# Moving two GpSimd memsets of a fused attention and MLP kernel to the wait for x, and fixing the order of its first layer-norm operations

## Chip, cores and metric

One NeuronCore of a Trainium2 chip. The metric is the device time of one execution in microseconds (us), lower is better. "Span" is the part of an execution that the profile covers; in every profiled run here it is 1.7 to 1.8 us shorter than the time. A run is called slow when it lies over 1.5% above the fastest of the same kernel; ratios use the fast runs alone.

## The reference, cut to what matters

```python
x = A_x                                   # 1 x 2048 x 448, bf16
xn = layernorm(x)
s = linear_attention(xn, wqkv, wo)        # 16 heads of 28
g = silu((relu(xn @ w1 + b1) ** 2) @ w2 + b2)
return x + s * g
```

## The kernel before

The kernel builds a list of operations with their dependencies and estimated durations. A list scheduler then chooses the order on VectorE (DVE), ScalarE (ACT) and GpSimd (POOL); the order on TensorE (PE) and on the DMA-issuing queue of SyncE (SP) is that of the program. Every engine's program then holds its list in that order, with semaphores to wait on.

To start PE before the layer norm is known, the first eight tiles of `x @ w1` use raw x. The norm is applied afterwards, by adding a small matmul (the "augmenting" matmuls, L901) to their accumulators. Its operands are statistics rows, made on VectorE:

```python
        pr.hot = -100.0                  # rising priorities for this group
        for si in range(4):
            ln_stats(si)                 # L511 bn_stats, L513 bn_aggr
        stat_rows()                      # L844, L851, L864, L868: the rows; ACT: rstd, sdev
        ln(0, 4, stats=False, rstd=False)  # L537 normalise, L546 copy, DMA transposes of xn
        pr.hot = None
# ... (cut)
        rt = row_transpose()             # PE transposes rows, L892 copies them to SBUF
# ... (cut)
        aug([H0[i] for i in range(4)], range(4), True)      # L901
# ... (cut)
        load_k("sp", w_qkv, A_wqkv, "wq", 0, D)   # SP queue, behind the first transposes
        load_w1(3, "sp", "sp")
        load_x(8, 12)                    # x for tiles 8 to 11: VectorE waits for it later
        ln(4, 8, lead=3, hold=[rt])
```

GpSimd meanwhile writes constants. `hmask` and `kvm` are needed only in the last third of the kernel, `ehd` too:

```python
        def late_constants():
            hv = hmask[:, :].rearrange("p (b j) -> p b j", b=HC)
            pool(lambda e, _: e.memset(hv, 1.0), ["hmask"])
            # ... two affine_selects on hmask; zmask: one memset, eight affine_selects (cut)
            pool(lambda e, _: e.memset(kvm[:, :, :], 0.0), ["kvm"], dur=1.0)   # 128 x 1792 bf16
            pool(lambda e, _: e.memset(ehd[:, :], 0.0), ["ehd"], dur=0.5)
            # ... four affine_selects on ehd, 128 x 448 bf16 each (cut)
```

Of the kernel before, what the change touches and what calls it, by code (L numbers as in the profile page):

```python
# [28 lines left out]
class Op:  # L29
    def __init__(self, eng, emit, reads, writes, dur, alts, nbytes):  # L30
        self.eng, self.emit, self.dur, self.alts, self.nbytes = eng, emit, dur, alts, nbytes
        self.reads, self.writes = list(reads), list(writes)
        self.raw, self.deps, self.succ = set(), set(), []
        self.start = self.end = None
        self.seq = None
        self.late = 1e9
        self.prio = None
        self.sync = None
        self.fence = False
        self.fixed = 0.0  # L40
        self.hold = ()


class Program:
# [14 lines left out]
    def add(self, eng, emit, reads=(), writes=(), dur=0.2, alts=(), nbytes=0):  # L59
        reads = [p for r in reads for p in self.aliases.get(r, (r,))]  # L60
        op = Op(eng, emit, reads, writes, dur, alts, nbytes)
        op.lead = self.lead
        if self.hot is not None:
            self.hot += 0.01
            op.prio = self.hot
        for t in op.reads:
            w = self.writer.get(t)
            if w is not None:
                op.raw.add(w)
            self.readers.setdefault(t, []).append(op)  # L70
        for t in op.writes:
            w = self.writer.get(t)
            if w is not None and w is not op:
                op.deps.add(w)
            for r in self.readers.get(t, ()):
                if r is not op:
                    op.deps.add(r)
            self.writer[t] = op
            self.readers[t] = [r for r in self.readers.get(t, ()) if r is op]
        op.raw.discard(op)  # L80
        op.deps |= op.raw
        for d in op.deps:
            d.succ.append(op)
        self.ops.append(op)
        return op

    def schedule(self):
# [29 lines left out]
        pend = {e: [] for e in self.ENGINES}  # L117
# [4 lines left out]
        def ready(op):  # L122
            r = 0.0
            for d in op.deps:
                if d.end is None:
                    return None
                r = max(r, d.end + LAT)
            for d in op.hold:
                if d.end is None:
                    return None  # L130
                r = max(r, d.start)
            return r
# [14 lines left out]
        while n:  # L147
            best = None
            for e in self.ENGINES:
                if e in fixed:  # L150
                    if not pend[e]:
                        continue
                    op = pend[e][0]
                    r = ready(op)
                    if r is None:
                        continue
                    new = [b for b in op.writes if isinstance(b, Buf) and b.bank is None]
                    banks = []
                    if new:
                        times = sorted(  # L160
                            (bank_time(b), b) for b in range(PSUM_BANKS) if bank_time(b) is not None
                        )
                        if len(times) < len(new):
                            continue
                        banks = [b for _, b in times[: len(new)]]
                        r = max(r, times[len(new) - 1][0])
                    st = max(r, free[e])
                    cand = (st, 0, op, e, banks, op.dur)
                else:
                    cands = []  # L170
                    for op in pend[e]:
                        r = ready(op)
                        if r is not None:
                            cands.append((max(r, free[e]), op))
                    for o in ops:
                        if o.end is None and o.alts:
                            for ae, ad in o.alts:
                                if ae == e:
                                    r = ready(o)
                                    if r is not None:  # L180
                                        cands.append((max(r, free[e]), o))
                    keep = []
                    for st, op in cands:
                        if op.alts:
                            mine = op.dur if op.eng == e else dict(op.alts)[e]
                            others = [(op.eng, op.dur)] + list(op.alts)
                            r = ready(op)
                            if any(
                                max(r, free[x]) + dx < st + mine - 1e-9 for x, dx in others if x != e
                            ):  # L190
                                continue
                            keep.append((st, op, mine))
                        else:
                            keep.append((st, op, op.dur))
                    if not keep:
                        continue
                    m = min(keep, key=lambda k: k[0])
                    st, op, du = min(
                        (k for k in keep if k[0] <= m[0] + min(0.6 * m[2], 0.02 + max(0.0, 0.3 * (m[1].late - k[1].late)))),
                        key=lambda k: k[1].late,  # L200
                    )
                    cand = (st, 1, op, e, [], du)
                if best is None or cand[0] < best[0] - 1e-12:
                    best = cand
            st, _, op, e, banks, du = best
            if op.eng != e:
                pend[op.eng].remove(op)
                op.eng = e
            else:
                pend[e].remove(op)  # L210
            for b, k in zip([b for b in op.writes if isinstance(b, Buf) and b.bank is None], banks):
                b.bank = k
                if bank_last[k] is not None:
                    self.bankdeps.setdefault(op, []).extend(users[bank_last[k]])
                bank_last[k] = b
            op.start = st
            if op.fixed:
                free[e] = st + op.dur
                op.end = st + op.dur + op.fixed
            elif op.nbytes:  # L220
                free[e] = st + op.dur
                s2 = max(dma_free, st + 1.9)
                dma_free = s2 + op.nbytes / 330e3
                op.end = dma_free + 0.7
            else:
                op.end = st + du
                free[e] = op.end
            order[e].append(op)
            n -= 1
# [63 lines left out]
def bass_recurrent_scan__linear_attn_block__dense_activation_squared_relu__prompt_kernel(  # L293
    nc, A_x, A_wqkv, A_wo, B_x, B_w1, B_b1, B_w2, B_b2, out
):
    with ExitStack() as es:
# [3 lines left out]
        add = pr.add  # L300
# [4 lines left out]
        hmask = sb("hmask", [P, PD], f32)  # L305
# [51 lines left out]
        def pool(fn, writes, reads=(), dur=0.3):  # L357
            add("pool", fn, reads, writes, dur)
# [45 lines left out]

        def late_constants():
            hv = hmask[:, :].rearrange("p (b j) -> p b j", b=HC)
            pool(lambda e, _: e.memset(hv, 1.0), ["hmask"])
            select(hv, "hmask", [[-DH, HC], [0, DH]], 0, 1, 0.0)
            select(hv, "hmask", [[DH, HC], [0, DH]], DH - 1, -1, 0.0)
            pool(lambda e, _: e.memset(zmask[:, :, :], 1.0), ["zmask"])  # L410
            for view, pat, base in (
                (zmask[:, 0:3, :], [[P, 3], [-DH, 32]], 0),
                (zmask[:, 3, :], [[-DH, 32]], 384),
                (zmask[:, 4, :], [[-DH, 32]], 320),
            ):
                select(view, "zmask", pat, base, 1, 0.0)
                select(view, "zmask", [[-a, n] for a, n in pat], DH - 1 - base, -1, 0.0)
            select(zmask[:, 3, :], "zmask", [[0, 32]], 63, -1, 0.0)
            select(zmask[:, 4, :], "zmask", [[0, 32]], -64, 1, 0.0)
            pool(lambda e, _: e.memset(ones[:, :], 1.0), ["ones"], dur=0.1)  # L420
            pool(lambda e, _: e.memset(kvm[:, :, :], 0.0), ["kvm"], dur=1.0)
            pool(lambda e, _: e.memset(ehd[:, :], 0.0), ["ehd"], dur=0.5)
            ev = ehd[:, :].rearrange("p (h j) -> p h j", h=NH)
            for g in range(NG):
                select(ev, "ehd", [[-1, NH], [0, DH]], -32 * g, 1, 1.0, ALU.not_equal, dur=0.6)
# [958 lines left out]
```

## Time and profile before

| | before |
|---|---|
| time, median | 150.86 us of 3 runs (150.5 to 150.94); with one more run 150.71 |
| span of the profile | 149.6 us (that execution took 151.34 us) |
| PE busy | 96% of the span |
| first operation on the statistics rows, L844 | 1.72 us for 128x32 elements |
| augmenting matmuls, L901 | start at 12.43 us |
| first transposes of xn on the SP queue | issued at 11.37 us |
| first matmuls of the second weight, L1106 | start at 38.62 us |

The profiled execution was slower than the median of the kernel's other executions.

The page of the profile of before: the span, the busy times, and PE and VectorE in 40 slices of 3.7 us, in tenths.

```profile
span 149.6 us, 2937 instructions
PE 143.4 (96%) x1164; PEld 71.4 (48%) x1165; DVE 99.7 (67%) x232; ACT 79.2 (53%) x149; POOL 37.2 (25%) x56
...
PE   7998998999899999999999999999999999999990
...
DVE  3799749999988899647999701059693616226353
```

PE, busy for 96% of the span, is the bound, so only its gaps can be won. The view of who waited for whom, for PE (time in total, times, longest):

```profile
PE pb L1223 <- DVE bsel L380: 1.1, 1, 1.1
PE pb L901 <- DVE scr L892: 0.7, 1, 0.7
PE pb L665 <- ACT pqT L643: 0.6, 1, 0.6
PE pb L1106 <- DVE r L722: 0.5, 1, 0.5
```

The timeline of VectorE (start, duration, engine, line, operation, out<-in):

```profile
8.13 1.72 DVE L844 TENSOR_SCALAR rows<-mv 128x32 bf16<-128x32 f32 x1
9.88 0.23 DVE L851 SCALAR_TENSOR_TENSOR rows<-mv,rows 128x16 bf16<-128x16 f32 x1
9.98 0.19 DVE L864 CAST rows<-sdev 128x16 bf16<-128x16 f32 x1
10.06 0.48 DVE L537 TENSOR_SCALAR xn<-x_tok,mv,rstd 128x448 bf16<-128x448 bf16 x1
10.46 0.21 DVE L868 TENSOR_TENSOR rows<-sdev,rows 128x16 bf16<-128x16 f32 x1
...
22.47 0.63 DVE L511 BATCH_NORM_STATS2 st<-x_tok 128x6 f32<-128x448 bf16 x1 [2.02 <-DMA x_tok<-in_A_x_dram]
...
36.81 1.75 DVE L722 TENSOR_TENSOR r<-r 128x512 bf16<-128x512 bf16 x5
```

and of GpSimd:

```profile
8.20 1.59 POOL L421 MEMSET kvm<- 128x1792 bf16 x1
```

L844 runs from 8.13 to 9.85, the memset from 8.20 to 9.79. That an operation of only 32 elements takes 1.72 us and ends 0.06 us after a memset on another engine suggests that it was waiting for it. At 22.47 VectorE had waited 2.02 us for the load of x's tiles 8 to 11. The SP queue shows why that load comes late; it is the fourth group behind the first transposes, and the queue has hardly a gap:

```profile
11.37 2.72 SPq L551 DMA_TRANSPOSE xT<-xn  x2
14.13 1.79 SPq L430 DMA_DIRECT2D w_qkv<-in_A_wqkv_dram  x3
15.96 0.59 SPq L430 DMA_DIRECT2D w<-in_B_w_dram  x1
16.60 1.76 SPq L430 DMA_DIRECT2D w_1r<-in_B_w_dram  x2
18.40 0.58 SPq L430 DMA_DIRECT2D x_tok<-in_A_x_dram  x1
```

### The profile page before, as it was taken

The page shows a single profiled execution, that of the slowest core. Times are in us where ns is not written, and L with a number is a line of the kernel's source. Part 1 is how long each engine was busy: PE and PEld are TensorE (multiplying, and loading weights), DVE is VectorE, ACT ScalarE, POOL GpSimd, SP SyncE. Part 2 cuts the span into 40 slices and gives each one's busy share as a digit, 9 for nine tenths or more (in the row PEclk, how much of TensorE's full clock was granted, in tenths as well). Part 3 has the DMA queues.
Part 4 walks back from the last instruction along what each step waited for, and adds up shares of the span by engine and source line. Part 5 has one row for each costly group of instructions (what it writes and reads, how often), then busy time and mean ns, then how long its engine had stood idle before and what let it go on. Part 6 is the DMA issues. An engine that isn't in the chain of part 4 may idle for free.

```text
span 149.6 us, 2937 instructions
## 1 busy us (share of the span) xinstructions
PE 143.4 (96%) x1164; PEld 71.4 (48%) x1165; DVE 99.7 (67%) x232; ACT 79.2 (53%) x149; POOL 37.2 (25%) x56
## 2 busy tenths in 40 slices
PE   7998998999899999999999999999999999999990
PEld 7962443554344445444444454454444544545450
DVE  3799749999988899647999701059693616226353
ACT  1525889679876796078969822897511020310200
POOL 7870023255000155000550000000000917208100
PEclk9999999999999999999999999999999999999999
DMA  4996889991330650000000000000000110201112
GB/s 119 330 288 127 197 183 216 334 326 36 67 73 0 40 105 0 0 0 4 0 2 4 2 0 0 4 0 0 0 0 4 61 61 32 91 4 61 61 61 61
DMA packets 17995, 11.06 MB, mean 74 GB/s; under 512 B 9469, under 2 KB 17597, under 8 KB 17982
## 3 DMA queue, kind: packets, MB, share of 16 engines
q1 hardware_dynamic: 17420, 10.42, 28.5%
q10 hardware_dynamic: 562, 0.46, 0.9%
q8 instruction: 9, 0.15, 0.4%
q14 instruction: 4, 0.03, 0.1%
HBM read 6.95 MB, written 1.84 MB: 59 GB/s over the span
## 4 chain that ended last, share of the span: by engine, by line
PE 84%; DVE 12%; ACT 2%; issue 0%; DVEq 0%
PE pb L1106 29%; PE pb L746 19%; PE pb L665 6%; PE pb L920 6%; PE pb L687 6%; PE pb L1173 6%; PE pb L1223 3%; DVE xn L537 3%; DVE r L722 2%; PE pb L745 2%; DVE pk L655 2%; PE pb L1209 1%; DVE rows L844 1%; PE pb L926 1%; PE pb L1006 1%; DVE pk L648 1%
## 5 line engine op out<-in xcount | busy, mean ns | idle before, releaser
L1106 PE MATMUL pb<-w,r 128*128 128x448 bf16 x224 | 44.3, 353 | 0.5 <-DVE r L722 0.5
L746 PE MATMUL pb<-xT,w 64*128 64x512 bf16 x288 | 37.8, 376 | 0.0
L717 ACT ACTIVATE r<-pb,b1f 128x512 bf16<-128x512 f32 x48 | 30.1, 691 | 6.5 <-PE pb L746 6.4
L1106 PEld LDWEIGHTS pb<-w,r 128*128 128x128 bf16 x224 | 21.1, 98 | 21.7 <-issue 2.2
L675 POOL TENSOR_TENSOR zacc<-zacc,pk 128x448 f32<-128x448 f32 x13 | 14.4, 1105 | 41.4 <-DVE pk L655 38.1
L1146 ACT ACTIVATE gbuf<-gbuf 128x448 bf16<-128x448 bf16 x15 | 8.5, 581 | 29.7 <-DVE gbuf L1136 29.7
L1162 POOL TENSOR_TENSOR obuf<-obuf,x_tok 128x448 bf16<-128x448 bf16 x12 | 12.0, 1035 | 48.6 <-DVE obuf L1156 48.6
L746 PEld LDWEIGHTS pb<-xT,w 64*128 64x128 bf16 x288 | 14.3, 94 | 16.1 <-issue 0.4
L722 DVE TENSOR_TENSOR r<-r 128x512 bf16<-128x512 bf16 x35 | 17.4, 532 | 2.3 <-ACT r L717 2.2
L1136 DVE TENSOR_TENSOR gbuf<-pb,b2b 128x448 bf16<-128x448 f32 x11 | 6.9, 625 | 13.7 <-PE pb L1106 13.6
L1156 DVE TENSOR_TENSOR obuf<-pb,gbuf 128x448 bf16<-128x448 f32 (+2 forms) x17 | 9.4, 592 | 7.3 <-PE pb L1173 4.7
L665 PE MATMUL pb<-w_qkv,xT 64*128 64x448 bf16 x112 | 13.3, 349 | 0.6 <-ACT pqT L643 0.6
L1089 DVE TENSOR_TENSOR pqT<-pqT,pb 128x512 bf16<-128x512 bf16 x12 | 7.4, 680 | 8.6 <-PE pb L1066 8.6
L723 ACT ACTIVATE r<-r 128x512 bf16<-128x512 bf16 x21 | 12.6, 637 | 0.0
L511 DVE BATCH_NORM_STATS2 st<-x_tok 128x6 f32<-128x448 bf16 x16 | 9.1, 611 | 3.2 <-DMA x_tok<-in_A_x_dram 3.2
L687 PE MATMUL pb<-xT,w_qkv 64*128 64x512 bf16 x84 | 11.0, 376 | 0.0
L655 DVE SCALAR_TENSOR_TENSOR pk<-pb,pk 128x448 bf16<-128x448 f32 x16 | 9.8, 622 | 0.4
L643 ACT ACTIVATE pk<-pb 128x448 bf16<-128x448 f32 x16 | 7.8, 541 | 4.0 <-PE pb L665 4.0
L920 PE MATMUL pb<-pk,xn 128*128 128x448 bf16 x48 | 9.4, 353 | 0.0
L746 PE MATMUL pb<-xT,w_1r 64*128 64x512 bf16 x48 | 9.2, 376 | 0.0
L665 PEld LDWEIGHTS pb<-w_qkv,xT 64*128 64x128 bf16 x112 | 5.5, 94 | 6.6 <-ACT pqT L643 1.0
L655 DVE SCALAR_TENSOR_TENSOR pqT<-pb,pqT 128x512 bf16<-128x512 f32 x12 | 8.2, 689 | 0.3
(122 smaller groups left out, 143.7 us busy)
## 6 DMA issues: line engine op xcount, KB each, us to landing
out_dram<-obuf SPq DMA_DIRECT2D x15, 112.0 KB, 1.7
w<-in_B_w_dram SPq DMA_DIRECT2D x1, 1568.0 KB, 8.7
x_tok<-in_A_x_dram SPq DMA_DIRECT2D x3, 448.0 KB, 4.6
w_qkv<-in_A_wqkv_dram SPq DMA_DIRECT2D x3, 336.0 KB, 6.4
w<-in_B_w_dram SPq DMA_DIRECT2D x2, 384.0 KB, 5.7
x_tok<-in_A_x_dram SPq DMA_DIRECT2D x2, 224.0 KB, 3.1
w_o<-in_A_wo_dram SPq DMA_DIRECT2D x1, 392.0 KB, 8.0
w<-in_B_w_dram ACTq DMA_DIRECT2D x1, 384.0 KB, 4.5
```

The lines of the kernel that those rows point to most:

```text
L655: lambda e, _: e.scalar_tensor_tensor(out=slot, in0=ps(buf)[:, 0:n], scalar=1.0 + 1e-6, in1=slot, op0=ALU.add, op1=ALU.max),
L665: return e.matmul(ps(b)[:, 0:D], xT[rw, si, c, :], w_qkv[rw, c, D : 2 * D], start=start, stop=stop)
L675: lambda e, _: e.tensor_tensor(out=o[:, :], in0=pk[:, 0, :] if i == 1 else zacc[:, :], in1=pk[:, i, :], op=ALU.add),
L687: return e.matmul(ps(b)[:, 0:512], w_qkv[rw, c, m * P : (m + 1) * P], xT[rw, 4 * g : 4 * g + 4, c, :], start=start, stop=stop,)
L717: rl = lambda e, _: e.activation(out=slot, in_=ps(b)[:, 0:512], func=AF.Relu, bias=b1f[:, fi : fi + 1])
L722: return e.tensor_tensor(out=slot, in0=slot, in1=slot, op=ALU.mult)
L723: return e.activation(out=slot, in_=slot, func=AF.Square)
L746: return e.matmul(ps(b)[:, 0:512], lhs, xT[rw, 4 * g : 4 * g + 4, c, :], start=start, stop=stop)
L920: last = e.matmul(ps(b)[:, 0:D], xn[:, si, c * P : (c + 1) * P], pk[:, si, :], start=(si == 0), stop=(si == NT - 1),)
L1106: last = e.matmul(ps(bb[fi >= 8])[:, 0:D], r2[:, fi, si * P : (si + 1) * P], w_2[:, fi, :], start=(fi == 0 and part is None) or (g == 0 an ...
L1156: "dve", lambda e, _: e.tensor_tensor(out=ob, in0=ps(b)[:, 0:w], in1=gs, op=ALU.mult),
L1162: lambda e, _: e.tensor_tensor(out=ob, in0=ob, in1=x_tok[:, si, lo:hi], op=ALU.add),
```

## The change

The intent: the kvm memset (1.59 us) and hmask's memset should run while VectorE still waits for x. A second part, the "rank" rule, makes VectorE and ScalarE take the operations of the first group in program order. Before, the scheduler could pass one by another.

```diff
+        self.rank = None
...
         if self.hot is not None:
             self.hot += 0.01
-            op.prio = self.hot
+            op.prio = op.rank = self.hot
...
+                    first = min((o.rank for o in pend[e] if o.rank is not None), default=None)
                     for op in pend[e]:
-                        r = ready(op)
+                        r = ready(op) if op.rank is None or op.rank == first else None
...
-            pool(lambda e, _: e.memset(hv, 1.0), ["hmask"])
+            add("pool", lambda e, _: e.memset(hv, 1.0), [], ["hmask"], 0.2).prio = -40.0
...
-            pool(lambda e, _: e.memset(kvm[:, :, :], 0.0), ["kvm"], dur=1.0)
+            add("pool", lambda e, _: e.memset(kvm[:, :, :], 0.0), [], ["kvm"], 1.0).prio = -50.0
```

The change adds two lines, so L844 of before is L846 of after, L901 is L903, L1106 is L1108, and so on. The text keeps the numbers of before.

## The prediction

> **What bounds the kernel now.** The page gives PE 96% busy of a 149.6 us span, and its slices show PE at 8 to 9 tenths from the first slice to the last but one. So the time changes only by PE's idle gaps. The view of PE's waits lists four: 1.1 us at the start (warm-up matmuls wait for a VectorE memset), 0.7 us at 12.43 (the augmenting matmuls, L901, wait for the VectorE copy of the transposed statistics rows, L892), 0.6 us at 25.10 (a bank that ScalarE has to empty), 0.5 us at 38.62 (L1106 waits for VectorE's squares, L722). The chain of waits in order of time runs on VectorE without a break from 6.39 to 12.38 and hands to L901 at 12.43: only here can the change act directly.
>
> **The suspect.** In that chain the first row operation (L844, 128x32 elements) takes 1.72 us, 8.13 to 9.85. Its neighbours of 128x16 take 0.19 to 0.23. GpSimd's memset of kvm (128x1792 bf16) runs 8.20 to 9.79, 1.59 us: the row operation ends 0.06 us after it. [...] about 1.5 us of the row operation is waiting. Likewise L537 (normally 0.39 us) has one of 1.19 us at 34 to 36.9, beside GpSimd adds of 1.1 us.
>
> **What the change moves.** The kvm memset, and hmask's (0.19 us), go to about 1.8 us, behind ident, rows and eps5, which the priorities still put first. They end at about 3.6, about when the first x tile's statistics begin (3.49). The tiny L393 (0.24 us at 1.83) will probably be held by the memset until about 3.4, and the statistics start 0.1 to 0.2 later: free, as VectorE then idles 1.1 us before 5.97. The zmask and ehd selects slide by about 1.8 us and now lie beside the row operations, until about 10.4. I think they hold VectorE little: L537 at 10.06 took 0.48 beside a hmask select, 0.09 over its usual time.
> The rank rule puts each aggregation behind its statistics and the last row operation before the first normalisation. I estimate 0.1 us lost for each of two dependent pairs.
>
> **On the critical path.** The first row operation falls to about 0.25 us. VectorE's rows and normalisations come about 1.3 us earlier. But PE is busy until 11.77 with work that doesn't need them (col sums, tails, row transposes at 10.73, L745), and csl waits for a ScalarE copy that ends at 10.64. L901 then starts at about 11.8 instead of 12.43: of 1.5 us saved on VectorE, 0.65 us reaches PE. The first transposes of xn are issued at about 10.1 instead of 11.37, so the SP queue, back to back from there to past 25 us, and the x loads behind it come about 1 us earlier (VectorE waits 2.0 us for one at 22.47). That may take some tenths off the gap at 38.62. Everything else shifts along.
>
> **Prediction.** 150.86 - 0.65 - 0.15 = 150.05 us; 8 in 10: 149.3 to 150.8. Faster by over 2%: 0.03; within 2%: 0.96; slower: 0.01.
>
> **Signs.** L844 at 0.2 to 0.4 us; kvm's memset over before 3.7; L393 over 1 us; PE's 0.7 us wait for L892 gone or under 0.1; L901 near 11.8; SP's first transposes near 10.1; the gap at 38.62 not over 0.5.
>
> **What would make it wrong.** The ehd selects (0.67 us each) holding L844, L851 and the normalisations as the memset did, which gives the gain back; the altered VectorE order moving a later square or bank release; the gap at 38.62 growing by what was won, because VectorE's load from 28 to 38 us sets it.

The sum is 150.86 less 0.65 for L901 and 0.15 for the earlier load of x, 150.05. The "about 1.5 us" of waiting is the estimate, the 1.72 us of L844 less the 0.19 to 0.23 us of its neighbours.

## The result, and the profile after

| | before | after |
|---|---|---|
| time, median | 150.71 us of 4 runs (150.5 to 150.94) | 150.12 us of 4 runs (149.97 to 150.45) |
| ratio after / before | | 0.9964, 95% interval 0.994 to 0.9988 |
| the same ratio (e6 below, chip 9) | | 0.997, interval 0.9947 to 0.9993 |
| span of the profile | 149.6 | 148.4 |
| L844, L864 | 1.72, 0.19 us | 0.72, 0.67 us |
| L901 starts | 12.43 | 11.98 |
| first transposes issued | 11.37 | 10.91 |
| L1106 starts | 38.62 | 37.42 |

A ratio is the mean time of one kernel's fast runs over that of the other's of the same rounds, so it isn't quite the ratio of the medians that are quoted.

The page of after:

```profile
span 148.4 us, 2936 instructions
PE 143.2 (97%) x1164; PEld 71.6 (48%) x1165; DVE 100.8 (68%) x231; ACT 79.5 (54%) x150; POOL 37.2 (25%) x56
...
PE   7999999999999999999999999999999999999990
...
DVE  6899859899988899458999510069683617226343
```

What PE waited for:

```profile
PE pb L1225 <- DVE bsel L382: 1.1, 1, 1.1
PE pb L903 <- DVE scr L894: 0.3, 1, 0.3
PE pb L1108 <- issue: 0.2, 1, 0.2
```

VectorE:

```profile
1.83 1.91 DVE L395 TENSOR_SCALAR rm<-ident 128x4 f32<-128x4 bf16 x1 [0.25 <-POOL eps L378]
...
8.29 0.72 DVE L846 TENSOR_SCALAR rows<-mv 128x32 bf16<-128x32 f32 x1
9.05 0.23 DVE L853 SCALAR_TENSOR_TENSOR rows<-mv,rows 128x16 bf16<-128x16 f32 x1
9.15 0.67 DVE L866 CAST rows<-sdev 128x16 bf16<-128x16 f32 x1
9.86 0.23 DVE L870 TENSOR_TENSOR rows<-sdev,rows 128x16 bf16<-128x16 f32 x1
...
21.44 0.63 DVE L513 BATCH_NORM_STATS2 st<-x_tok 128x6 f32<-128x448 bf16 x1 [1.47 <-DMA x_tok<-in_A_x_dram]
...
35.91 1.42 DVE L724 TENSOR_TENSOR r<-r 128x512 bf16<-128x512 bf16 x4
```

GpSimd:

```profile
1.78 1.59 POOL L423 MEMSET kvm<- 128x1792 bf16 x1
...
6.67 3.10 POOL L370 TENSOR_SCALAR_AFFINE_SELECT ehd<-ehd 128x448 bf16<-128x448 bf16 x4
```

The SP queue:

```profile
10.91 2.80 SPq L553 DMA_TRANSPOSE xT<-xn  x2
...
17.39 0.59 SPq L432 DMA_DIRECT2D x_tok<-in_A_x_dram  x1
```

The hold of the memset is gone from the rows. But the affine selects of ehd, which slid from 5.0 to 8.1 us into 6.7 to 9.8 us, now lie beside them: L844 takes 0.72 us and L864 0.67 us, about 0.5 us each over their free times (0.20 us each, e11 below). The third select ends at 8.96 and L844 at 9.01, the fourth at 9.77 and L864 at 9.82: the same sign as with the memset. The memset now holds the tiny L393 instead, for 1.91 us, which costs nothing here. Two gaps of PE beyond those of the rows closed too: the 0.6 us at 25.10, and most of the 0.5 us at 38.62.

### The profile page after: what moved, and what is told of

Its sections match the earlier page's. It is cut to its first block, busy times and chain, and to the rows that moved or that the text cites. A ratio compares the mean times of both kernels' runs of the same rounds, so it can differ in the third digit from the quotient of the medians.

```text
span 148.4 us, 2936 instructions
## 1 busy us (share of the span) xinstructions
PE 143.2 (97%) x1164; PEld 71.6 (48%) x1165; DVE 100.8 (68%) x231; ACT 79.5 (54%) x150; POOL 37.2 (25%) x56
## 4 chain that ended last, share of the span: by engine, by line
PE 84%; DVE 8%; DMA 3%; SPq 2%; issue 1%; ACT 0%; DVEq 0%
PE pb L1108 29%; PE pb L748 22%; PE pb L922 6%; PE pb L1175 6%; PE pb L689 5%; PE pb L667 5%; PE pb L1225 3%; DMA x_tok<-in_A_x_dram 3%; DVE st L513 3%; SPq L432 2%; PE pb L704 1%; PE pb L1211 1%; PE pb L928 1%; PE pb L1008 1%; DVE xn L539 1%; DVE pk L657 1%
## 5 line engine op out<-in xcount | busy, mean ns | idle before, releaser
L1108 PE MATMUL pb<-w,r 128*128 128x448 bf16 x224 | 44.3, 353 | 0.2 <-issue 0.2
L1108 PEld LDWEIGHTS pb<-w,r 128*128 128x128 bf16 x224 | 21.1, 98 | 21.4 <-issue 2.6
L725 ACT ACTIVATE r<-r 128x512 bf16<-128x512 bf16 x22 | 13.3, 636 | 0.0
```

What stands on the lines that cost most here:

```text
L725: return e.activation(out=slot, in_=slot, func=AF.Square)
L1108: last = e.matmul(ps(bb[fi >= 8])[:, 0:D], r2[:, fi, si * P : (si + 1) * P], w_2[:, fi, :], start=(fi == 0 and part is None) or (g == 0 an ...
```

## The experiments

Three theories. T: a GpSimd instruction holds VectorE's row operations, and moving the memset is the gain. R: the rank rule's new order is the gain. N: the waits were a chance of one profile. Kernels of one call ran on one chip: e1 to e4, e5 to e8, e9 to e12. All results were correct to the reference.

For reading all of them together, this table gives the milestones of the thirteen profiles that are of use (us from the span's start, read from the timelines): the first copy of transposed x by VectorE (L770), which marks how soon PE got going; L901; the issue of the first transposes; the end of VectorE's wait for x's tiles 8 to 11; L1106; and the span.

| profile | L770 | L901 | transposes | x there | L1106 | span |
|---|---|---|---|---|---|---|
| before | 5.97 | 12.43 | 11.37 | 22.47 | 38.62 | 149.6 |
| before, e5 | 5.65 | 12.40 | 11.35 | 22.33 | 38.53 | 149.5 |
| memsets only, e1 | 5.96 | 11.86 | 10.80 | 21.66 | 37.87 | 148.9 |
| memsets only, e9 | 5.12 | 11.22 | 10.18 | 21.32 | 37.56 | 148.5 |
| rank only, e2 | 5.20 | 12.04 | 10.99 | 21.46 | 37.40 | 148.4 |
| rank only, e10 | 5.42 | 12.02 | 10.96 | 21.87 | 37.78 | 148.8 |
| after | 5.96 | 11.98 | 10.91 | 21.44 | 37.42 | 148.4 |
| after, e6 | 5.77 | 11.56 | 10.52 | 21.42 | 37.33 | 148.3 |
| kvm split, e3 | 5.18 | 11.25 | 10.39 | 21.34 | 37.42 | 148.4 |
| kvm double, e4 | 5.02 | 13.08 | 12.03 | no wait | 40.15 | 151.1 |
| deferred, e11 | 5.96 | 11.79 | 10.16 | 21.14 | 37.34 | 148.3 |
| deferred and rank, e12 | 5.93 | 11.53 | 10.07 | 20.96 | 36.88 | 147.8 |
| deferred, x early, e8 | 5.88 | 11.48 | 9.85 | 14.48 | 37.62 | 148.6 |

Three things stand in it. The rest of the span after L1106 is 110.9 to 111.0 us in every row: all that the variants do is decided by then. L1106 comes 16.1 to 16.2 us after x is there with the old order, and 15.9 to 16.0 us with the rank rule, in all rows but e4 and e8. And L770 itself varies from 5.02 to 5.97 us between executions.

The last comes from PE's rate. PE's first matmuls (the warm-up, L1223, and the transposes of x, L763) start 107 ns apart, and from some moment on 56 ns apart. That moment lay at 6.0 us in before and after, and near 3.8 us in e4 and e9 (an estimate from the starts of the groups: 38 warm-up matmuls from 1.05 us, and the first transpose at 4.49 and 4.46 us). In e11 it had not come when the last transpose of x started near 6.25 (an estimate: the twelfth start from 5.08 us on, at 107 ns). So the 12 transposes took 1.27 us in before and 0.83 us in e4, and the moment varies by over 2.4 us between executions. What sets it isn't shown. The granted clock doesn't show it: it is recorded as 1.00 from the first matmuls on, also where these start 107 ns apart (windows view of before, after and e1 to e4; the mean of the profiled executions of e9 and e11 is 1.0).

### e1 and e9: only the memsets

```diff
 # the kernel before, with
-            pool(lambda e, _: e.memset(hv, 1.0), ["hmask"])
+            add("pool", lambda e, _: e.memset(hv, 1.0), [], ["hmask"], 0.2).prio = -40.0
-            pool(lambda e, _: e.memset(kvm[:, :, :], 0.0), ["kvm"], dur=1.0)
+            add("pool", lambda e, _: e.memset(kvm[:, :, :], 0.0), [], ["kvm"], 1.0).prio = -50.0
```

> The kernel before with the two memsets moved and without the rank rule: only GpSimd's order changes, every other engine's order is that of before. Theory T (the memset holds the first row operation until it ends): L844 falls from 1.72 us to 0.2 to 0.8 us (it may still meet an ehd select of 0.67 us), L901 starts 0.3 to 0.7 us earlier than 12.43, the time is 0.3 to 0.8 us under the kernel before, which is all or nearly all of the gain of the change. Rival R (the gain comes from the rank rule's new order on VectorE): L844 is as short, but L901 stays within 0.2 us of 12.43 and the time within 0.2 us of before.

Measured: 150.59 us median (150.03 to 151.21), ratio to before 0.9991, interval 0.9961 to 1.0021. PE's wait before L901 is gone, as T expected:

```profile
8.23 0.20 DVE L844 TENSOR_SCALAR rows<-mv 128x32 bf16<-128x32 f32 x1
8.46 0.60 DVE L851 SCALAR_TENSOR_TENSOR rows<-mv,rows 128x16 bf16<-128x16 f32 x1
...
9.33 0.67 DVE L868 TENSOR_TENSOR rows<-sdev,rows 128x16 bf16<-128x16 f32 x1
```

Here the selects hit two other operations, each with two inputs: L851 took 0.60 us and L868 0.67, against 0.23 and 0.22 in e11. The time is not lower beyond its noise.

> e1 again, on the same chip as e10 to e12, since e1's interval (0.9961 to 1.0021) told nothing. Theory T: no operation of VectorE over 0.8 us before 12 us except L393; PE's wait before L901 under 0.2 us; ratio to before 0.994 to 0.998. Rival R (the rank rule is the cause): ratio 0.999 to 1.002.

Measured: 150.65 us median (150.17 to 151.11), ratio 1.000, interval 0.9977 to 1.0024. No row operation was over 0.7 us and PE's wait was 0.17 us, as T expected; but the ratio isn't what T expected. On the time, T's claim that the memsets alone bring the gain has failed twice. In profiles with the same start (L770 at 5.96 or 5.97) e1 still has a span 0.7 us shorter than before (148.9 against 149.6).

### e2 and e10: only the rank rule

```diff
 # the kernel after, with the two memset lines of before
-            add("pool", lambda e, _: e.memset(kvm[:, :, :], 0.0), [], ["kvm"], 1.0).prio = -50.0
+            pool(lambda e, _: e.memset(kvm[:, :, :], 0.0), ["kvm"], dur=1.0)
 # (hmask likewise)
```

> The kernel after with the two memsets put back where they were: VectorE, ScalarE, PE and SP have the order of after, GpSimd that of before. Theory T: L844 is 1.4 to 1.7 us again, ending about 0.06 us after the kvm memset; L901 at 12.2 to 12.6; the time within 0.2 us of the kernel before. Rival R: L844 as long, but L901 near 12.0 and the time 0.4 to 0.8 us under before.

Measured: 150.53 us median (150.03 to 151.02), ratio 0.9987, interval 0.9958 to 1.0015. The start was an early one, so the memset (8.25 to 9.84 us) met a later operation than L844. L844 took 0.72 us, and:

```profile
8.32 1.58 DVE L866 CAST rows<-sdev 128x16 bf16<-128x16 f32 x1
```

It ends at 9.90, 0.06 us after the memset. L901 came at 12.04, the figure of R, but PE had been ready 0.72 us earlier, as T says.

> e2 again, for the same reason. Theory T: one operation of VectorE ends within 0.1 us of the kvm memset's end (9.8 to 9.9) and takes over 1.5 us; PE's wait before L901 0.6 to 1.2 us; ratio to before 0.999 to 1.002. Rival R: ratio 0.994 to 0.998.

Measured: 150.63 us median (150.37 to 151.37), ratio 1.001, interval 0.9984 to 1.0037. Again the cast took 1.58 us, and PE waited 0.78 us for L901. R fails too: the rank rule alone brings no gain in time that is clear of its noise.

### e3: the memset in four pieces

```diff
-            pool(lambda e, _: e.memset(kvm[:, :, :], 0.0), ["kvm"], dur=1.0)
+            pool(lambda e, _: [e.memset(kvm[:, c, :], 0.0) for c in range(4)][-1], ["kvm"], dur=1.0)
```

> The kernel before, with the kvm memset issued as four instructions of 448 elements at the same place, about 0.45 us each, so GpSimd writes the same bytes at the same time. [...] L844 ends within 0.1 us of the end of the first or second piece, so it takes 0.4 to 1.0 us, and L901 comes 0.3 to 0.6 us earlier than before. If VectorE is only slowed for as long as GpSimd writes[...]: L844 stays at 1.5 us or over and L901 at about 12.4.

The first outcome there is that of T: L844 is held to the end of one piece. The other is that it is slowed or held through all four. The 0.45 us for a piece is an estimate; in before the memset of ehd, as long as a piece (448 elements), took 0.47 us.

Measured: 150.32 us median (149.88 to 150.97), ratio 0.9975, interval 0.9948 to 1.0002. In this early start L844 came before the memsets and took 0.20 us. So the forecast for L844 could not be tested. The first operations that met the four pieces took 0.66 us (L864) and 0.68 us (L537), the normalisations and the copy after them 0.50 to 0.62 us, each ending within 0.17 us of the end of a piece, if the four, from 8.20 to 10.31, are taken as equally long (an estimate; they were read as one group); nothing in the group was over 0.70 us, and L901 started at 11.25. GpSimd wrote the same bytes in 2.11 us instead of 1.59. So here no operation was held through the 2.11 us of all four; VectorE got its turns in between. The time is not clear of that of before.

### e4: a memset twice as long

```diff
-        kvm = sb("kvm", [P, 4, D], bf)
+        kvm = sb("kvm", [P, 8, D], bf)      # the memset covers all of it; only half is used
```

> The kernel before with a kvm tile twice as large, so its memset is one instruction of 3584 elements, about 3.15 us; all orders as before. T: L844 takes 3.2 to 3.4 us and ends 0.06 us after the memset; VectorE has no slack after it, so L901 comes about 1.5 us later, near 13.95, and the time rises by 1.2 to 1.7 us. If the row operation is not on the path of PE, L844 grows alike but L901 and the time move by under 0.5 us.

Measured: 152.65 us median (152.23 to 152.91), ratio 1.0124, interval 1.0099 to 1.0149: 1.9 us more. The start was early, so the memset (8.26 to 11.47) met not L844 but the second normalisation:

```profile
8.46 3.14 DVE L537 TENSOR_SCALAR xn<-x_tok,mv,rstd 128x448 bf16<-128x448 bf16 x1
```

usually 0.39 us. That is T, at twice the dose. L901 came at 13.08, only 0.65 us later than in before, but e4's start was early: in e9, with as early a start and no memset in the way, L901 came at 11.22, and in e2, with the memset of 1.59 us, at 12.04. Part of the time lost in the profiled execution is of another kind, which the windows view shows (stretch, PE busy, weight loads, VectorE, ScalarE, GpSimd, then the granted PE clock, DMA share, GB/s):

```profile
12.00:14.00 2.00, 0.92 (x7) 0.41 (x8) 2.00 (x6) 0.47 (x1) 0.16 (x1) 1.00 0.37 70
14.00:16.00 2.00, 2.00 (x7) 0.73 (x5) 2.00 (x9) 1.97 (x6) 0.00 (x0) 0.51 1.03 190
16.00:18.00 2.00, 2.00 (x13) 0.28 (x13) 1.67 (x7) 0.09 (x1) 0.00 (x0) 0.63 0.82 210
```

In this execution PE waited 2.13 us for L901; after that its granted clock was 0.51 from 14 to 16 us and 0.63 from 16 to 18 us, and the nine matmuls behind L901 took 3.42 us instead of 2.12 (e1). Not every execution had this: the mean granted clock was 0.987 and 0.986 in the two that took 152.9 us, but 1.000 in the two of 152.23 and 152.30 us. The latter are still about 1.6 us above the mean of before in the same call (150.71 us), within the 1.2 to 1.7 us that T expected; about 0.6 us of the slowest two goes with the clock.

### e5 and e6: before and after again

> The kernel before, unchanged: a placebo, and a second profile of it. The profiles so far show two starts: PE's matmuls reach full rate before 5 us (e2, e3, e4) or only near 6 us (before, after, e1). Time ratio to before 0.998 to 1.002. Theory T: [...] PE's wait before L901 is 0.6 to 0.8 us in a late start, 0.8 to 1.4 us in an early one. Rival N (the wait of 0.7 us was a chance of the one profile of before): it is under 0.3 us here.

What was to be measured: an operation of VectorE that is up when the memset starts at 8.20 ends with it at 9.8 to 9.9. "Full rate" is the 56 ns from start to start of above.

Measured: ratio of before to itself 1.0005, interval 0.9977 to 1.0032. N fails: the hold is there again, and PE waited 0.66 us for L901 and 0.33 us for the transposes of the rows before it.

```profile
7.72 2.10 DVE L844 TENSOR_SCALAR rows<-mv 128x32 bf16<-128x32 f32 x1
```

L844 came up 0.4 us earlier than in the first profile, while a select was running, and still ended at 9.82, 0.06 us after the kvm memset. It was held through three GpSimd instructions in a row: the select (to 8.11), the hmask memset (8.05 to 8.24) and the kvm memset (8.17 to 9.76).

> The kernel after, unchanged, for more times of it on the same chip as the others, and a second profile. Ratio to before 0.993 to 0.999, as in the first measurement (0.9964). Theory T: no VectorE operation longer than 0.75 us before 12 us except L393 near 2 us; PE's wait before L901 is 0.2 to 0.5 us in a late start and up to 0.8 us in an early one, at least 0.3 us less than before has in the same kind of start.

Measured: 150.36 us median (150.04 to 150.63), ratio 0.997, interval 0.9947 to 0.9993. No row operation is longer than 0.45 us, and PE doesn't wait for L901 at all.

### e7 and e11: all late constants out of the start

```diff
         def late_constants():
-            # hmask, kvm and ehd: memsets and affine_selects
             # zmask and ones stay
+        def deferred_constants():
+            after = [("pk", 11)]
+            pool(lambda e, _: e.memset(kvm[:, :, :], 0.0), ["kvm"], after, dur=1.6)
+            # hmask and ehd likewise, then their affine_selects
...
         for i in range(8, 12):
             zsum(i)
+        deferred_constants()
```

> The kernel before with the kvm memset and all work on hmask and ehd moved to GpSimd's idle time near 58 us, so after about 4.5 us GpSimd does nothing until its first add near 20 us. The order of every other engine is that of before, without the rank rule. Theory T [...]: L844, L851, L864, L868 take 0.19 to 0.25 us each, L537 0.38 to 0.40; PE's wait before L901 is under 0.1 us in either start; the time is 0.3 to 0.9 us under before. If the affine selects do no harm, the result is that of e1 (time within 0.2 us of e1's).

Measured: five runs of 149.19 to 150.64 us; ratio 0.9942, interval 0.991 to 0.9974. A sixth execution, the profiled one, took 833 us. In it the matmuls of L746 took 1697 ns instead of 377, and the 38 warm-up matmuls already 12.50 us instead of 4.23 (e11), with a granted clock of 1.00 in the records. It counts as slow and is left out; its cause is open.

> e7 again, as its profile fell on an execution of 833 us. No hold left: L844, L851, L864, L868 0.19 to 0.25 us each; PE's wait before L901 under 0.1 us; the first transposes issued 0.4 to 1.0 us earlier than in after; ratio to before 0.991 to 0.997, at or under after's 0.997. A second execution far over 160 us would mean that the kernel itself, and not that execution, is at fault.

Measured: 149.93 us median (149.06 to 150.34), ratio 0.9947, interval 0.9916 to 0.9977; no slow execution among the six. VectorE in the profile (this kernel's lines are 3 higher than those of before):

```profile
8.26 0.20 DVE L847 TENSOR_SCALAR rows<-mv 128x32 bf16<-128x32 f32 x1
8.50 0.23 DVE L854 SCALAR_TENSOR_TENSOR rows<-mv,rows 128x16 bf16<-128x16 f32 x1
8.83 0.20 DVE L867 CAST rows<-sdev 128x16 bf16<-128x16 f32 x1
8.93 0.40 DVE L540 TENSOR_SCALAR xn<-x_tok,mv,rstd 128x448 bf16<-128x448 bf16 x1
9.24 0.22 DVE L871 TENSOR_TENSOR rows<-sdev,rows 128x16 bf16<-128x16 f32 x1
```

These are the free times. The start was as late as that of before (L770 at 5.96), and all orders but GpSimd's are those of before; the first transposes go out 1.2 us earlier. VectorE's rows and the transposes gain more by this version than by the change. Whether the time does isn't shown: on e6's chip, e7's five fast runs have a mean of 149.98 us, e6's six 150.35 us (no interval was taken of these two). The holds are moved and not gone: six of VectorE's squares (L725) from 54.81 to 60.46 us, beside two adds of GpSimd and then the selects (56.92 to 60.20), take 5.65 us. In before seven squares, beside two adds alone, take 4.10 us. PE loses nothing by it, as the rest of the span after L1106 is unchanged.

### e8: the load of x earlier as well

```diff
 # e7, with
+        load_x(8, 12)          # ahead of the first group, where the SP queue is idle
         pr.hot = -100.0
...
-        load_x(8, 12)
```

> As e7, and x's tokens 8 to 11 of each row are loaded ahead of the first transposes, where the SP queue is idle (7.9 to 10.9 us), instead of behind seven other issues. If the next bound is that load's arrival (VectorE waited for it in every profile, 1.5 to 2.0 us near 21 us): the wait is gone, PE's waits near 25 and 38 us are gone, and the time is 0.3 to 0.8 us under e7. If PE does not depend on it: within 0.3 us of e7. It may be slower if the load delays the w_qkv or w_1 loads that PE needs near 14 us.

Measured: 150.28 us median (149.99 to 151.24), ratio 0.997, interval 0.9942 to 0.9998: not under e7 (its mean is 150.41 us, e7's 149.98), so the forecast of 0.3 to 0.8 us less failed. VectorE's wait near 21 us is gone, but PE's wait before L1106 is still 0.47 us, and the load, issued at 7.98 and there at 14.48, now overlaps the first transposes: issuing these, from 9.85 on, took 4.33 us instead of 3.09 (e11), and the first matmuls on transposed xn started at 15.41 after a gap of 0.63 us, against 15.03 without one in e11. The scheduler also changed the order on VectorE and ScalarE. So one bound may have been traded for another; which one decides isn't shown.

### e12: deferred, with the rank rule

The same edit as e7, on the kernel after.

> The kernel after with the kvm memset and the work on hmask and ehd at 58 us as in e7, so with the rank rule. If the rank rule has no effect of its own: within 0.3 us of e11. If it delays csl (L830 and L892 come behind two normalisations and a copy): PE's wait before L901 0.1 to 0.4 us longer than in e11.

Measured: 149.56 us median (149.21 to 150.74), ratio 0.9938, interval 0.9907 to 0.9969. PE doesn't wait for L901. Its mean of 149.66 us is 0.12 us under e11's 149.78, within noise. This is the lowest ratio found, though not clear of e11's or e7's; both deferred versions beat before by 0.5 to 0.6%.

## Why the prediction was right, and where not

**The time.** 150.05 us was predicted, with 149.3 to 150.8; 150.12 us came out. The gain was 0.59 us between medians, against 0.81 us predicted. That the two are so close is partly luck: errors of opposite sign met. The rows gained about 0.5 us of the 1.5 us expected, and L1106 came earlier by more than L901 did, in ways that the sum did not contain.

**The hold by the memset: right.** In each profile with the memset near 8.2 us, except e3's with its pieces, some operation of VectorE ends within about 0.15 us of the memset's end: L844 (before, e5), the cast (e2, e10), a normalisation (e4). With GpSimd idle the same operations take 0.20 to 0.40 us (e11). With the memset twice as long the time rose by 1.9 us (e4), and with no GpSimd instruction beside the rows it fell (ratios 0.9942 in e7, 0.9947 in e11). By what mechanism one engine's instruction holds the other's isn't shown. Nor is it when a waiting operation is passed over by the next GpSimd instruction: L844 waited 2.10 us through a select and two memsets in e5, and L393 1.91 us through three memsets in after, but in e3, with four in a row, VectorE got its turn in between.

**The selects: the step that failed.** The prediction said of the selects that slide beside the rows: "I think they hold VectorE little". It rested on one L537 that was 0.09 us over its usual time. In after they added about 0.5 us each to L844 and L864; in e1 they hit L851 and L868, in e9 L864 and L868. That gave back some 1.0 of the 1.5 us. The transposes went out at 10.91 (10.52 in e6) instead of the predicted 10.1, which the deferred versions reach (10.16 and 10.07), and e9 (10.18) only by its early start. The traces show the hold: the row operations that were held beside the selects of 0.67 us took 0.45 to 0.72 us (after, e1, e6, e9) instead of 0.20 to 0.23 us, and where the ends of the selects were read, the held one ends 0.05 to 0.07 us after one (L844 and L864 in after, L868 in e1). Not every operation beside them was held: in e1 L537, at 9.02, took its usual 0.39 us. Beside the memset, L868 took 0.21 us (e4) and L851 0.23 us (e2), so the two operations with two inputs were held by a select and not seen held by a memset. Why isn't shown.

**The way to the end: the terms were mis-assigned.** The prediction gave 0.65 us to PE's wait before L901 and 0.15 us to the earlier load of x. The profiles say otherwise. L901 moved by 0.45 us and L1106 by 1.20 us. In e9 PE waits 0.17 us for L901 against 0.66 us in before, but also about 0.3 us at each of three other places and 0.5 us before L1106, and the span follows L1106. What L1106 follows, to within 0.16 us for each of the two orders and in all eleven rows but e4 and e8, is the arrival of x's tiles 8 to 11; and this follows the issue of the first transposes by 10.5 to 11.1 us. So the hold seems to cost time mostly through the SP queue: late rows, late normalisation, late transposes, late x, VectorE behind until 38 us, PE's waits at 25 and 38 us. The wait at L901 is one that PE would otherwise have had later. This is read from the timelines. The one run that moved the load itself, e8, had x 6.7 us earlier than e11 and L1106 no earlier (37.62); but it also slowed the transposes and changed the order, so the link isn't isolated by an experiment. Nor is all of the 1.03 us by which x came earlier in after the work of the hold. The two issues of w_1r just ahead of that load took 1.76 us in before and 1.14 in after, which makes 0.62 us of it. They took 1.56 us in e5, but 1.14 in e2 and e10, where the memset held the rows as well. What lengthened them is open.

**The rank rule: a gain where a risk was seen.** Its forecast cost, 0.1 us for each of two dependent pairs, came: from the third tile's statistics to L844 it is 1.59 to 1.60 us with the rule (after, e2, e6, e12) and 1.39 without it (before, e9, e11). The prediction feared that "the altered VectorE order" would move a later square. It did, the good way. With the rank rule the scheduler gave one more square to ScalarE; VectorE's last group before L1106 holds four of them (1.42 us) instead of five (1.75 us), and L1106 comes 15.9 us after x instead of 16.2.

**Why neither half shows a gain by itself: partly open.** Both halves have ratios of 0.999 to 1.001, and the whole has 0.9964 and 0.997. The intervals of about 0.25 to 0.3% to either side are as wide as the effect, so a sum of two small gains isn't excluded, nor is an interaction shown. What blurs it is seen: the memset's end is fixed at about 9.8 us, and the start of L844 varies from 7.09 (e4) to 8.29 us (after) with the moment at which PE's first matmuls pass from 107 to 56 ns apart. An early start gets some rows done ahead of the memset. Runs of before spread from 150.02 to 151.38 us (33 runs), those of after from 149.97 to 150.63 us (10 runs). Both profiles of before fell on executions above 151.2 us, so the prediction's reading, like the pair of spans (149.6 to 148.4), shows more than the typical run loses. No early start of before was caught in a profile, so that its slow runs are the late starts is argued, not shown; the long issues of w_1r in both profiles of before are another candidate.

**The other signs.** L844 took 0.72 us in the first profile (predicted 0.2 to 0.4: wrong) and 0.20 in e6. The kvm memset was over at 3.37 (under 3.7: right). L393 took 1.91 us (over 1: right); it ended 0.3 us later than expected, at 3.74, 0.07 us after the second of the two memsets behind kvm's (3.67). The wait for L892 was 0.29 us in the first profile (predicted under 0.1) and none in e6. L901 at 11.98 and 11.56, predicted near 11.8. The gap before L1106 is 0.2 us, not over 0.5: right.

## What to carry to other kernels

When a tiny VectorE operation takes over a microsecond (here L844, 1.72 us), look for a GpSimd instruction that ends just before it (here the memset, by 0.06 us), and move every GpSimd instruction out of that stretch; moving only the longest let the others slide in here, at about 0.5 us on each of two operations. Then follow the freed operation not only to the engine that waits for it next but to the DMA queue that it feeds: here, as the timelines read, the queue's order carried the delay 27 us further. And take a second profile before believing a gap of half a microsecond, since the moment at which PE's matmuls pass from 107 to 56 ns apart, near 3.8 to over 6.25 us here, shifts what follows: the first copy of transposed x started at 5.02 to 5.97 us.
